# Softmax attention behind the last row maxima in cycles of two steps, with the output projections in parts between the cycles

## The chip, the cores and the metric

The kernel runs on one core of a Trainium2 chip. The metric is the device time of one execution in microseconds (us). A core has engines that run side by side and meet at semaphores: PE (matrix multiply, with weight loads shown apart as PEld), DVE (VectorE), ACT (ScalarE), POOL (GpSimd) and SP, which here issues the DMAs in one list. PE writes to PSUM, eight banks of 128 partitions by 512 float32; operands lie in SBUF.

## The reference

Two attention branches over one input of 2048 tokens and 448 channels, 16 heads of 28 channels, mixed by a gate for each token. All is float32.

```python
x = A_x
g = _sigmoid((x * gate_w).sum(-1, keepdims=True))
a = _A_ref(x, A_wqkv, A_w_phi, A_wo)     # linear attention with a softmax feature map
b = _B_ref(x, B_wqkv, B_wo)              # softmax attention
return g * a + (1 - g) * b

def _B_ref(x, wqkv, wo):
    ...
    scores = jnp.einsum("bhqd,bhkd->bhqk", q, k) * scale
    p = _softmax(scores, axis=-1)
    o = jnp.einsum("bhqk,bhkd->bhqd", p, v)
    return (lambda x, *d: x.transpose(*d))(o, 0, 2, 1, 3).reshape(B, S, D) @ wo
```

The change touches branch B alone, in its last part.

## The kernel before

The first half of the program makes branch A, the queries, keys and values of B, and the first part of the row maxima that the softmax subtracts. The second half is a loop over steps `s` from 0 to 255. The 16 heads go in four groups of four (`g`), the queries in four blocks of 512 (`qb`), the keys in 16 tiles of 128 (`kt`). One step is one `(g, qb, kt)`, with `gq = 4 g + qb` counting groups of 16 steps.

In a step, `scores` makes four score tiles of 128 keys by 512 queries, one for each head, each in a PSUM bank of its own (`st`); ACT takes the exponential of each into a tile `p` in SBUF. `values` of the step before multiplies the four `p` by the values and adds into one bank `pv`: four matmuls of 32 columns each, at four column positions of the array, each stands in the profile as two instructions. While maxima are still to be found, `mx_visit` does a piece of that work in each step: four matmuls `pm`, one ACT and some DVE instructions. It has work in steps 1 to 212. From then on the banks that it held join the rotation, and one, `spare`, is kept for projections, so that six banks remain for scores.

After the last step of a group `finish` normalises in parts that are put into later steps: `f1` copies `pv` (DVE) and gathers the denominators by DMA; `f2`, three steps on, takes the reciprocal and sends it through DRAM to all partitions (`rdb`, `rsb`); `f3`, eight steps on, multiplies (POOL); `f4` splits the result into a high and a low part (POOL, tile `oTb`). For the first three head groups the result goes to DRAM (`od`).

For the last head group, `g = 3`, steps 192 to 255, the output can be made: `project(qb, oT, tl)` makes 128 tokens of the output by 11 matmuls into the spare bank (`pob`): eight read `oL`, the results of the first three groups loaded back from DRAM by `load_out` (the first six read blocks 0 and 1, the next two block 2), and three read `oTb`. DVE adds that to branch A's part in `acc`, and a DMA writes it out. A query block has four projections, in the steps `s + 10` to `s + 13` behind its `finish` (dictionary `mids`). The loads of `oL` are put in steps 200, 222, 242 and 206 (`OUTS`, by query block). `oL` is one buffer for the first three query blocks; the fourth has its own. `acc` has two buffers. Query block 3 is projected at the end, behind the loop's last values, by code that the change leaves alone.

The order on PE, DVE, ACT and POOL is the order in which the program is written; the order of SP's DMAs is made by a planner. SP issues in order: a DMA that waits holds those behind it.

Of the kernel before, what the change touches and what calls it, by code (L numbers as in the profile page):

```python
# [8 lines left out]
F32 = mybir.dt.float32  # L9
# [8 lines left out]
P = 128  # L18
S = 2048
D = 448  # L20
# [3 lines left out]
NG = 4  # L24
NT = S // P
NQ = S // 512
# [2 lines left out]
NU = NG * NQ * 16  # L29
NF = 44  # L30
LOWEST = -3.0e38
OUTS = (200, 222, 242, 206)


def f32(ap):
    return ap.bitcast(F32)
# [3 lines left out]
def gated_mix_kernel(ctx, tc, xT, wqkB, wvB, wvA, wkAT, wqAT, phi, woA, woB,  # L40
# [7 lines left out]
    nc = tc.nc  # L48
# [18 lines left out]
    def ps_mx(nm, d):  # L67
        return ps.tile([P, 2, 512], F32, tag="md" if d and psn[1] == 3 else "mx", name=nm,
                       bufs=1 if d and psn[1] == 3 else 2)
# [18 lines left out]
    gate1 = const.tile([P, NT], F32, name="gate1")  # L88
# [17 lines left out]
    def run(dst, todo):  # L106
        for i, (l, r) in enumerate(todo):
            nc.tensor.matmul(dst, l, r, start=i == 0, stop=i == len(todo) - 1)  # L108
# [48 lines left out]
    acts = []  # L157
# [6 lines left out]
    def take_acts():  # L164
        while acts:
            acts.pop(0)()
# [11 lines left out]
    def mx_tile(tag, nm, bufs):  # L178
        return mxp.tile([P, 512], F32R, tag=tag, name=nm, bufs=bufs)
# [49 lines left out]
    def mx_fin():  # L229
        while mxs["fin"]:  # L230
            mxs["fin"].pop(0)()
# [162 lines left out]
    def normalize1(pool, pn, nm, n):  # L394

        oU = pool.tile([P, n, 512], F32, tag="oU", name=f"oU{nm}", bufs=1 + n)
        for i in range(n):
            (nc.scalar.copy if n == 2 else nc.vector.tensor_copy)(oU[:, i, :], pn[i])  # L398
        den = pool.tile([P, n, 16], F32, tag="den", name=f"den{nm}", bufs=2)
        for i in range(n):  # L400
            nc.sync.dma_start(den[:, i, :], oU[DH:P:32, i, :])
        return oU, den

    def normalize2(pool, oU, den, nm, n, eps):

        if eps:
            nc.vector.tensor_scalar_add(den, den, EPS)
        nc.vector.reciprocal(den, den)
        rd = dr.tile([4, n * 512], F32, tag=f"rd{n}", name=f"rd{nm}", bufs=2)
        rs = pool.tile([P, n, 512], F32, tag="rs", name=f"rs{nm}", bufs=2)  # L410
        for k in range(n):
            nc.sync.dma_start(rd[:, k * 512:(k + 1) * 512], den[:, k, :])
        nc.sync.dma_start(rs.rearrange("p n q -> p (n q)"),
                          rd.unsqueeze(1).to_broadcast([4, 32, n * 512]))
        return oU, rs

    def normalize3(oU, rs, n):

        (nc.gpsimd if n == 1 else nc.vector).tensor_mul(oU, oU, rs)  # L419
        return oU  # L420

    def normalize4(pool, oU, nm, n):

        oTn = []
        for k in range(n):
            oT = pool.tile([P, 2, 512], F32R, tag="oT", name=f"oT{nm}_{k}", bufs=2 * n)
            (nc.scalar.copy if n == 2 else nc.gpsimd.tensor_copy)(oT[:, 0, :], oU[:, k, :])
            nc.gpsimd.tensor_sub(oT[:, 1, :], oU[:, k, :], f32(oT[:, 0, :]))
            oTn.append(oT)
        return oTn  # L430

    def out_passes(oT, c, w, g):
        tt = slice(c, c + P)
        return [(oT[:, 0, tt], w[:, 0, g, :]), (oT[:, 0, tt], w[:, 1, g, :]),
                (oT[:, 1, tt], w[:, 0, g, :])]
# [270 lines left out]
    for i in range(2 * NT + 11):  # L706
        t, q = i, i - NT
# [131 lines left out]
        kst_of[(g, kb)] = load_stack(kst[(4 * g + kb) % 5], k_d[g], kb * 512, (0, 1, 0, 1))  # L839

    NS = NG * NQ * NT
    pv_of, pts, late, mids = {}, {}, {}, {}

    def scores(s, i):

        gq, kt = divmod(s, NT)
        g, qb = divmod(gq, NQ)

        def score(j, st):
            nc.tensor.matmul(st, kst_of[(g, kt // 4)][:, j, (kt % 4) * P:(kt % 4 + 1) * P],  # L850
                             qst_of[gq][:, j, :], start=True, stop=True)

        if s == 0:
            p = at.tile([P, 2, 512], F32, name=f"p{s}_{i}")
            st = ps_mx(f"st{s}_{i}", i)
            for jl in range(2):
                score(2 * i + jl, st[:, jl, :])
            nc.scalar.activation(p, st, AF.Exp, scale=SCALE)
            pts.setdefault(s, []).extend([p[:, 0, :], p[:, 1, :]])
            return  # L860
        sts = []
        for j in (2 * i, 2 * i + 1):
            used.append(free.pop(0))
            sts.append(bank(used[-1], f"st{s}_{j}"))
            score(j, sts[-1])
        for st in sts:
            p = late_p.tile([P, 512], F32, tag="p", name=f"p{s}_{len(pts.get(s, []))}", bufs=8)
            nc.scalar.activation(p, st, AF.Exp, scale=SCALE)  # L868
            pts.setdefault(s, []).append(p)
        if i == 1:  # L870
            a, m = used[:], held[:]
            free.extend([a[0], m[0], a[1], m[1], a[2], a[3], m[2]] if m else a)
            used.clear()
            held.clear()
# [34 lines left out]
    spare = []  # L909

    def bank(i, nm):
        return ps2.tile([P, 512], F32, tag=f"g{i}", name=nm, bufs=1)
# [13 lines left out]
    late_p = ctx.enter_context(tc.tile_pool(name="late", bufs=1, reuse_waits="tile"))  # L926
    woB_s = late_p.tile([P, 2, 4, D], F32R, name="woB_s")
# [51 lines left out]
                             start=kt == 0, stop=kt == NT - 1, tile_position=(0, 32 * j),  # L979
                             skip_group_check=True)  # L980

    def project(qb, oT, tl):

        t = qb * 4 + tl
        acc = acc_of[qb][:, tl, :]
        po = bank(spare[0], f"pob{t}")
        run(po[:, :D], first_passes(qb, tl) + out_passes(oT, tl * P, woB_s, NG - 1))
        nc.vector.scalar_tensor_tensor(acc, po[:, :D], gate1[:, t:t + 1], acc,  # L988
                                       op0=ALU.mult, op1=ALU.add)
        nc.sync.dma_start(out[0, t * P:(t + 1) * P, :], acc)  # L990

    def first_passes(qb, tl):
        o, tt = oL_of[qb], slice(tl * P, (tl + 1) * P)
        return [x for b in range(2) for x in out_passes(o[b], tl * P, woB_s, b)] + [
            (o[2][:, i, tt], woB_s[:, i, 2, :]) for i in range(2)]
# [18 lines left out]
    def finish(gq, s):  # L1014

        st = {}
        g, qb = divmod(gq, NQ)
        last = gq == NG * NQ - 1

        def f1():  # L1020
            st["n"] = normalize1(late_p, [pv_of[gq]], f"b{gq}", 1)

        def f2():
            st["n"] = normalize2(late_p, *st["n"], f"b{gq}", 1, False)

        def f3():
            st["n"] = normalize3(*st["n"], 1)

        def f4():
            st["o"], = normalize4(late_p, st["n"], f"b{gq}", 1)  # L1030
            if g < NG - 1:
                for j in range(4):
                    r = (4 * g + j) * DH
                    nc.sync.dma_start(o_d[r:r + DH, :, qb * 512:(qb + 1) * 512],
                                      f32(st["o"][32 * j:32 * j + DH]))

        if last:
            finish_last(gq)
            return
        f1()  # L1040
        late.setdefault(s + 3, []).append(f2)
        late.setdefault(s + 8, []).append(f3)
        late.setdefault(s + 9, []).append(lambda: acts.append(f4))
        if g == NG - 1:
            for tl in range(4):
                mids[s + 10 + tl] = lambda tl=tl: project(qb, st["o"], tl)

    def finish_last(gq):

# [44 lines left out]
    for s in range(NS + 16):  # L1094
        take_acts()
        if s < NS:
            gq, kt = divmod(s, NT)
            g, qb = divmod(gq, NQ)
            if s in (0, 3):
                load_k(0, 2 + s // 3)  # L1100
            if g + 1 < NG and qb == NQ - 1 and kt % 4 == 2:
                load_k(g + 1, kt // 4)
            if kt == 12 and gq + 1 < NG * NQ:
                load_q(gq + 1)
            if kt == (12 if gq + 1 < 14 else 14) and gq + 1 < NG * NQ - 1:
                load_nm(gq + 1)
            if s in OUTS:
                load_out(OUTS.index(s))
            if g == NG - 1 and kt == 8:
                load_acc(qb)  # L1110
            if s:
                scores(s, 0)
                scores(s, 1)
        if s == NS:
            tail_open()
            tail_fill(3)
        if 0 < s <= NS:
            values(s - 1)
            if s % NT == 0:
                finish(s // NT - 1, s)  # L1120
        if s:
            mx_visit()
        if mxs["f"] == len(flats):
            mx_fin()
        if s in mids:
            mids.pop(s)()
        if mxs["f"] == len(flats) and not spare:
            spare_open()
        if NG * NQ - 1 in nm_of and NG * NQ - 1 in qst_of:
            load_nm(NG * NQ - 1)  # L1130
        for fn in late.pop(s, []):
            fn()
# [68 lines left out]
```

## Time and profile before

| | |
|---|---|
| timed runs, us | 1028.92, 1027.72, 1028.66 (median 1028.66) |
| profiled execution, span, us | 1027.1 |
| median less that span, us | 1.56 |
| PE busy, us | 1018.7 |
| ACT busy, us | 819.4 |
| DVE busy, us | 672.8 |
| POOL busy, us | 245.1 |
| mean granted TensorE clock | 0.998 |

The page has the time of the profiled execution as its span, from the first to the last instruction; the timed runs hold some time around it. A line of the timeline has the start and the length in us, the engine, the line of the kernel, the operation, the tiles as out<-in, the shapes, and the number of instructions merged into it; behind it in brackets is the idle time of that engine before it and what ended that. A line of a table of windows has, for each engine, the busy us and the number of instructions, then the clock, the DMA share and GB/s. Matmuls overlap, so their starts tell more than their lengths.

### The profile page before, as it was taken

The page shows a single profiled execution, that of the slowest core. Times are in us where ns is not written, and L with a number is a line of the kernel's source. Part 1 is how long each engine was busy: PE and PEld are TensorE (multiplying, and loading weights), DVE is VectorE, ACT ScalarE, POOL GpSimd, SP SyncE. Part 2 cuts the span into 40 slices and gives each one's busy share as a digit, 9 for nine tenths or more (in the row PEclk, how much of TensorE's full clock was granted, in tenths as well). Part 3 has the DMA queues.
Part 4 walks back from the last instruction along what each step waited for, and adds up shares of the span by engine and source line. Part 5 has one row for each costly group of instructions (what it writes and reads, how often), then busy time and mean ns, then how long its engine had stood idle before and what let it go on. Part 6 is the DMA issues. An engine that isn't in the chain of part 4 may idle for free.

```text
span 1027.1 us, 17751 instructions
## 1 busy us (share of the span) xinstructions
PE 1018.7 (99%) x6344; PEld 561.2 (55%) x6344; DVE 672.8 (65%) x1335; ACT 819.4 (80%) x1534; POOL 245.1 (24%) x213
## 2 busy tenths in 40 slices
PE   8999999999999999999999999999999999999998
PEld 7878888878779433333333333333333333354545
DVE  5466566997750578888878788787878887710102
ACT  5354445687753899999999999999999999969672
POOL 1226456688436302111011110101201101011010
PEclk9999999999999999999999999999999999999999
DMA  8873110132245703233633123522313355414311
GB/s 294 292 243 116 42 34 19 43 90 79 91 129 122 158 19 83 65 71 68 127 70 77 46 66 81 129 57 50 87 46 74 87 131 138 124 56 127 122 42 54
DMA packets 64025, 98.88 MB, mean 96 GB/s; under 512 B 17952, under 2 KB 24720, under 8 KB 63936
## 3 DMA queue, kind: packets, MB, share of 16 engines
q1 hardware_dynamic: 63936, 97.74, 35.4%
q8 instruction: 50, 0.82, 0.4%
q14 instruction: 39, 0.32, 0.1%
HBM read 69.54 MB, written 27.78 MB: 95 GB/s over the span
## 4 chain that ended last, share of the span: by engine, by line
PE 95%; DVE 2%; DMA 1%; ACT 1%; issue 0%; SPq 0%; DVEq 0%; ACTq 0%
PE st L850 29%; PE pv L977 25%; PE pm L321 9%; PE pqk L108 5%; PE poa L108 4%; PE pk L126 4%; PE pva L126 4%; PE pob L108 3%; PE pq L108 3%; PE pvb L108 2%; PE pmb L284 2%; PE pvb L126 2%; PE pn L532 1%; PE pft L520 1%; PE pkv L475 1%; PE poL L1011 1%
## 5 line engine op out<-in xcount | busy, mean ns | idle before, releaser
L868 ACT ACTIVATE p<-st 128x512 f32<-128x512 f32 x1020 | 525.9, 609 | 29.5 <-PE st L850 27.8
L332 DVE TENSOR_REDUCE part<-pm 128x1 f32<-128x512 f32 x477 | 304.6, 685 | 131.5 <-PE pm L321 124.9
L850 PE MATMUL st<-qst,kst 128*128 128x512 f32 x1024 | 315.6, 430 | 0.5 <-ACT vb L694 0.5
L977 PE MATMUL pv<-p,vb 128*32 128x512 f32 x2048 | 272.8, 605 | 0.2 <-DVE oUb L398 0.2
L850 PEld LDWEIGHTS st<-qst,kst 128*128 128x128 f32 x1024 | 173.1, 187 | 137.4 <-issue 75.8
L321 PEld LDWEIGHTS pm<-kc,qc 28*128 28x128 f32 x848 | 40.5, 181 | 177.8 <-ACT p L868 169.4
L325 ACT ACTIVATE rl<-pm 128x512 f32<-128x512 f32 x212 | 126.9, 599 | 11.1 <-PE pm L321 0.3
L419 POOL TENSOR_TENSOR oUb<-oUb,rsb 128x512 f32<-128x512 f32 x15 | 19.4, 1291 | 469.2 <-DMA rsb<-rdb 375.1
L329 DVE CUSTOM_DVE_ANT_0 rl<-pm,rl 128x512 f32<-128x512 f32 x159 | 108.2, 680 | 0.0
L321 PE MATMUL pm<-kc,qc 28*128 28x512 f32 x848 | 107.1, 495 | 0.0
L289 DVE CUSTOM_DVE_ANT_0 rl<-pmb,rl 128x512 f32<-128x512 f32 x88 | 57.1, 686 | 32.4 <-ACT rl L287 32.4
L977 PEld LDWEIGHTS pv<-p,vb 128*32 128x32 f32 x2048 | 40.3, 108 | 67.6 <-issue 63.4
L988 DVE SCALAR_TENSOR_TENSOR acc<-pob,gate,acc 128x448 f32<-128x448 f32 x12 | 8.2, 683 | 86.2 <-PE pob L108 86.2
L108 PE MATMUL pqk<-XH,wB 128*128 128x512 f32 x192 | 60.8, 404 | 2.3 <-DVE ev L572 2.3
L287 ACT ACTIVATE rl<-pmd 128x1024 f32<-128x1024 f32 x44 | 45.3, 1029 | 8.0 <-ACT z_s L485 2.4
L571 ACT CAST ev<-pqk 128x512 fp32r<-128x512 f32 x28 | 16.0, 589 | 40.2 <-PE pqk L108 35.7
L108 PE MATMUL poa<-woA_s,oTa 128*128 128x448 f32 x192 | 43.2, 374 | 0.0
L108 PEld LDWEIGHTS pqk<-XH,wB 128*128 128x128 f32 x192 | 36.0, 192 | 11.4 <-DVE ev L572 2.7
L572 DVE TENSOR_TENSOR ev<-pqk,ev 128x512 fp32r<-128x512 f32 x28 | 19.0, 690 | 31.6 <-ACT ev L571 31.5
L108 PEld LDWEIGHTS poa<-woA_s,oTa 128*128 128x128 f32 x192 | 35.0, 188 | 5.8 <-issue 2.8
L195 POOL TENSOR_TENSOR kc<-kc,kd 28x512 fp32r<-28x512 f32 x12 | 15.4, 1282 | 95.7 <-DMA kc<-qkd 59.4
L126 PE MATMUL pk<-wkA_s,XH 128*128 128x448 f32 x128 | 37.9, 377 | 0.0
(155 smaller groups left out, 1186.6 us busy)
## 6 DMA issues: line engine op xcount, KB each, us to landing
qkd<-ev SPq DMA_DIRECT2D x28, 512.0 KB
qst<-qkd SPq DMA_DIRECT2D x64, 224.0 KB
kst<-qkd SPq DMA_DIRECT2D x64, 224.0 KB
od<-oTb SPq DMA_DIRECT2D x48, 112.0 KB
rsa<-rda SPq DMA_DIRECT2D x8, 512.0 KB
rsb<-rdb SPq DMA_DIRECT2D x15, 256.0 KB
kc<-qkd SPq DMA_DIRECT2D x64, 56.0 KB
gad<-ga SPq DMA_DIRECT2D x16, 224.0 KB
```

What stands on the lines that cost most here:

```text
L108: nc.tensor.matmul(dst, l, r, start=i == 0, stop=i == len(todo) - 1)
L126: nc.tensor.matmul(dst[:, :n], l, r, start=i == 0, stop=i == len(todo) - 1, skip_group_check=True)
L284: nc.tensor.matmul((pb if j < 2 else pd)[:, j % 2, :], qc[js, qt * P:(qt + 1) * P], kc[js, :], start=True, stop=True, tile_position=(32 * ...
L287: nc.scalar.activation(rl, pd, AF.Relu)
L289: nc.vector.tensor_tensor_reduce(rl[:, i, :], pb[:, i, :], rl[:, i, :], 1.0, LOWEST, ALU.add, ALU.max, part[:, col + i:col + i + 1])
L321: nc.tensor.matmul(pm[j], mxs[("qc", gq)][js, qt * P:(qt + 1) * P], mxs[("kc", g, kb)][js, :], start=True, stop=True, tile_position=(32 * ...
L325: nc.scalar.activation(rl, pm[kb], AF.Relu if kb < 3 else AF.Copy)
L329: nc.vector.tensor_tensor_reduce(r, pm[j], r, 1.0, LOWEST, ALU.add, ALU.max, part[:, col + j:col + j + 1])
L332: nc.vector.tensor_reduce(part[:, col + j:col + j + 1], pm[j], AX.X, ALU.max)
L850: nc.tensor.matmul(st, kst_of[(g, kt // 4)][:, j, (kt % 4) * P:(kt % 4 + 1) * P], qst_of[gq][:, j, :], start=True, stop=True)
L868: nc.scalar.activation(p, st, AF.Exp, scale=SCALE)
L977: nc.tensor.matmul(pv[32 * j:32 * j + 32, :], vb[kt // 8][:, kt % 8, 4 * g + j, :], pt[j], start=kt == 0, stop=kt == NT - 1, tile_position ...
```

## The change

From step `TWO` = 213 on, which is the first without work on maxima, steps go in pairs. In an odd step the scores of that step and of the next are made, eight in a row; then come the values of the step before it, and then, in the even step, the values of the odd one. The exponentials of even steps go to tiles that held queries and keys for the maxima (`qc`, `kc`), so that there are 16 tiles `p`.

A projection is cut into two halves, of six and of five matmuls into the same bank. They stand in a list, `halves`, with the earliest step for each, and are taken in even steps behind the values: one in a step up to 232, two in a step from 234 on. The earliest step is that behind `f4`, or three behind the load of `oL`. Those loads move from steps 222 and 242 to 233 and 243. For groups that end behind step 213, `f2`, `f3` and `f4` come 2, 5 and 6 steps behind the group's end instead of 3, 8 and 9.

```diff
-OUTS = (200, 222, 242, 206)
+OUTS = (200, 233, 243, 206)
...
+    TWO = NG * NQ * 16 - NF + 1
...
-        for st in sts:
-            p = late_p.tile([P, 512], F32, tag="p", name=f"p{s}_{len(pts.get(s, []))}", bufs=8)
+        for j, st in enumerate(sts, 2 * i):
+            if s < TWO or s % 2:
+                p = late_p.tile([P, 512], F32, tag="p", name=f"p{s}_{j}", bufs=8)
+            else:
+                tag = "qc" if s % 4 and j < 3 else "kc"
+                p = f32(mx_tile(tag, f"p{s}_{j}", 3 if tag == "qc" else 5))
...
-    def project(qb, oT, tl):
+    halves, po_b = [], {}
+
+    def project(qb, st, tl, half):
...
-        po = bank(spare[0], f"pob{t}")
-        run(po[:, :D], first_passes(qb, tl) + out_passes(oT, tl * P, woB_s, NG - 1))
-        nc.vector.scalar_tensor_tensor(acc, po[:, :D], gate1[:, t:t + 1], acc,
+        if half == 0:
+            po_b[t] = bank(spare[0], f"pob{t}")
+        todo = first_passes(qb, tl) + out_passes(st["o"], tl * P, woB_s, NG - 1)
+        for i, (l, r) in enumerate(todo):
+            if i // 6 == half:
+                nc.tensor.matmul(po_b[t][:, :D], l, r, start=i == 0, stop=i == 10,
+                                 skip_group_check=True)
+        if half == 0:
+            return
+        nc.vector.scalar_tensor_tensor(acc, po_b.pop(t)[:, :D], gate1[:, t:t + 1], acc,
                                        op0=ALU.mult, op1=ALU.add)
...
-        late.setdefault(s + 3, []).append(f2)
-        late.setdefault(s + 8, []).append(f3)
-        late.setdefault(s + 9, []).append(lambda: acts.append(f4))
+        d2, d3, d4 = (3, 8, 9) if s < TWO else (2, 5, 6)
+        late.setdefault(s + d2, []).append(f2)
+        late.setdefault(s + d3, []).append(f3)
+        late.setdefault(s + d4, []).append(lambda: acts.append(f4))
         if g == NG - 1:
-            for tl in range(4):
-                mids[s + 10 + tl] = lambda tl=tl: project(qb, st["o"], tl)
+            halves.extend((max(s + d4 + 1, OUTS[qb] + 3), lambda tl=tl, half=half: project(qb, st, tl, half))
+                          for tl in range(4) for half in range(2))
...
-            if s:
-                scores(s, 0)
-                scores(s, 1)
+            for z in ([s] if s < TWO else [s, s + 1][:NS - s] if s % 2 else []):
+                if z:
+                    scores(z, 0)
+                    scores(z, 1)
...
-        if s in mids:
-            mids.pop(s)()
+        for _ in range(0 if s % 2 else 1 if s < 234 else 2):
+            if halves and halves[0][0] <= s:
+                halves.pop(0)[1]()
```

More of the change, by code (lines that the diff above doesn't have):

```diff
@@ L841, in gated_mix_kernel @@
     NS = NG * NQ * NT
-    pv_of, pts, late, mids = {}, {}, {}, {}
+    TWO = NG * NQ * 16 - NF + 1
+    pv_of, pts, late = {}, {}, {}
     def scores(s, i):
```

## The prediction

> **What bounds the kernel now.** I read the page's first and fourth parts, then the chain of waits cut to the end of the run, where every edit lies, then the timeline there.
>
> ```profile
> PE 1018.7 (99%) x6344; PEld 561.2 (55%) x6344; DVE 672.8 (65%) x1335; ACT 819.4 (80%) x1534; POOL 245.1 (24%) x213
> PE 95%; DVE 2%; DMA 1%; ACT 1%; issue 0%; SPq 0%; DVEq 0%; ACTq 0%
> by line: PE st L850 34.9%; PE pv L977 33.2%; PE pob L108 19.9%; PE poL L1011 4.8%; PE poL L1080 1.7%; PE pm L321 1.5%; PE pr L1065 0.7%; PE pd L1055 0.7%; DVE oUb L398 0.5%; DVE acc L1081 0.5%; issue 0.1%
> ```
>
> The third line is the chain from 880 us on: scores (`st`), values (`pv`) and projections (`pob`), all on PE. A busy PE need not be full, so next the timeline of plain steps, with scores and ACT's exponentials also cut out singly:
>
> ```profile
> 898.08 1.06 PE L977 MATMUL pv<-p,vb 128*32 128x512 f32 x8
> 898.53 0.61 PE L977 MATMUL pv<-p,vb 128*32 128x512 f32 x4
> 899.08 0.76 PEld L850 LDWEIGHTS st<-qst,kst 128*128 128x128 f32 x4 [0.84 <-issue]
> 899.08 1.19 PE L850 MATMUL st<-qst,kst 128*128 128x512 f32 x4
> 899.41 0.39 PE L850 MATMUL st<-qst,kst 128*128 128x512 f32 x1
> 899.64 0.40 PE L850 MATMUL st<-qst,kst 128*128 128x512 f32 x1
> 899.88 0.40 PE L850 MATMUL st<-qst,kst 128*128 128x512 f32 x1
> 900.20 1.06 PE L977 MATMUL pv<-p,vb 128*32 128x512 f32 x8
> 899.67 0.60 ACT L868 ACTIVATE p<-st 128x512 f32<-128x512 f32 x1
> ```
>
> A step is 2.12 us (898.08 to 900.20): values 1.00 (to 899.08), scores 1.12. The scores' starts show where time is lost: 0.33 from the first to the second, 0.23 to each further one, and 0.32 from the fourth to the first value. In a run of scores each costs 0.23; so going from values (column tiles of 32) to scores costs 0.10 and back 0.09. The values are two lots of four that run side by side, 0.45 apart (898.08, 898.53), and the second needs 0.55 (to 899.08), though a lot of such width needs less inside a run. The nearest run of column tiles is `pn`, half as wide:
>
> ```profile
> 198.16 0.59 PE L532 MATMUL pn<-fT,KV 112*64 112x256 f32 x3
> 198.58 0.39 PE L532 MATMUL pn<-fT,KV 112*64 112x256 f32 x2
> ```
>
> These are its second and fourth lot: 0.42 for two lots of 256, so 0.43 (they stand at 0.215 each) for one of 512. Leaving the values thus costs 0.55 - 0.43 = 0.12. Does ACT bound instead? The steps with a projection:
>
> ```profile
> 905.44 1.89 PE L108 MATMUL pob<-woB_s,oL 128*128 128x448 f32 x8
> 907.78 1.08 PE L850 MATMUL st<-qst,kst 128*128 128x512 f32 x4
> 908.27 2.07 ACT L868 ACTIVATE p<-st 128x512 f32<-128x512 f32 x4 [2.29 <-PE st L850]
> 908.79 1.06 PE L977 MATMUL pv<-p,vb 128*32 128x512 f32 x8
> 909.79 1.90 PE L108 MATMUL pob<-woB_s,oL 128*128 128x448 f32 x8
> ```
>
> Four exponentials take 2.07, the last 0.60 alone, so they follow each other at 0.49; four are 1.96 of a 2.12 step. PE bounds, with ACT 8% behind it. A projection step is 4.35 (905.44 to 909.79): projection 2.34, scores 1.01 (no switch of tiles before them), values 1.00; ACT idles 2.29. So the stretch from step 213 on is 42 steps of 2.12 plus 12 projections of 2.23, all PE.
>
> **The change part by part.**
>
> *Eight scores, then two steps' values.* This removes one pair of switches per two steps. There are 21 cycles (213/214 to 253/254; 255 stays alone). Without waits a cycle's scores take 0.33 + 6 x 0.23 + 0.32 = 2.03 to 2.05, its values 0.45 + 2 x 0.43 + 0.55 = 1.86: 3.91 instead of 4.24.
>
> But the change adds a wait: `spare` leaves six banks in rotation, so the seventh and eighth score reuse the banks of the first and second and wait for their exponentials. The nearest row is a score that waits for ACT today:
>
> ```profile
> 892.75 0.60 ACT L325 ACTIVATE rl<-pm 128x512 f32<-128x512 f32 x1
> 893.40 0.19 PEld L850 LDWEIGHTS st<-qst,kst 128*128 128x128 f32 x1 [0.21 <-ACT rl L325]
> 893.82 0.16 PEld L977 LDWEIGHTS pv<-p,vb 128*32 128x32 f32 x8 [0.24 <-issue]
> ```
>
> ACT ends at 893.35, the weight load starts 0.05 later, the values 0.42 after that. In a cycle the first exponential starts 0.59 after the first score (899.08 to 899.67), the second ends at 0.59 + 0.49 + 0.60 = 1.68, the eighth's load starts at 1.73, the values at 2.15. Behind the waiting score stand only the values of the step before, ready long since. The seventh is released at 0.59 + 0.60 + 0.05 = 1.24, about when its load is due: no cost. So a cycle is 2.15 + 1.86 = 4.01, a gain of 0.23. After a projection all starts come 0.10 earlier: 2.05 + 1.86 + 2.34 = 6.25 against 2.12 + 4.35 = 6.47, gain 0.22. Bounds: 0.33 with no wait; 0.10 if lots stay 0.45 apart and the wait costs 0.08 more. The second half of the values needs the fourth exponential, at 0.59 + 3 x 0.49 + 0.60 + 0.05 = 2.71; it is due at 2.15 + 0.88 = 3.03. ACT's eight take 3.92 of 4.01. I take 0.225 x 21 = 4.7.
>
> *Values of a new group* stand behind eight scores instead of four. At step 240 they waited:
>
> ```profile
> 970.00 1.19 PE L850 MATMUL st<-qst,kst 128*128 128x512 f32 x4
> 970.61 0.69 DVE L398 COPY oUb<-pv 128x512 f32<-128x512 f32 x1 [5.99 <-PE st L850]
> 971.35 0.16 PEld L977 LDWEIGHTS pv<-p,vb 128*32 128x32 f32 x8 [0.60 <-DVE oUb L398]
> ```
>
> 1.35 from the scores instead of 1.12: 0.2 that goes. Next late behind it are the eight scores, 2.15.
>
> *Projections in two parts.* A part of six or five matmuls stands between values and scores: it pays the 0.10 of leaving the values, which the scores after it then save. Net 0, and the eight projections from step 236 on run both parts together, 2.34 as now. *More p tiles* (16 for 8): ACT's idle time in the rows is put down to `st`, not to a missing tile: 0.
>
> *The loads of `oL`.* Projections now run later and in longer rows, and `oL` is one buffer: the second query block's is loaded when the first's eighth half (step 232) has read it, and used at step 236. Before, 13 steps lay between; now two cycles. The same point before (920.86 is the first score behind the fourth projection, T in what follows):
>
> ```profile
> 920.44 0.60 SPq L942 DMA_DIRECT2D oL<-od  x1
> 920.86 1.09 PE L850 MATMUL st<-qst,kst 128*128 128x512 f32 x4
> 921.77 0.33 SPq L990 DMA_DIRECT2D out_dram<-acc  x1
> 922.15 0.58 SPq L942 DMA_DIRECT2D oL<-od  x1
> 922.78 1.20 SPq L945 DMA_DIRECT2D oL<-od  x2
> 924.96 0.42 SPq L948 DMA_DIRECT2D oL<-od  x1
> 928.75 0.47 SPq L968 DMA_DIRECT2D acc<-gad  x1
> 930.38 0.34 SPq L412 DMA_DIRECT2D rdb<-denb  x1
> 934.11 0.58 SPq L413 DMA_DIRECT2D rsb<-rdb  x1
> ```
>
> The built order of the changed program puts SP's issues here as: `oL` block 0, `out`, block 1, first part of block 2, `acc` (896 KB, for the third query block), then the other four parts of block 2 (346 KB). That `acc` takes the buffer of the first query block, so it waits until the `out` before it has landed, and the four parts stand behind it on SP. `out` is issued at T + 0.9 behind 512 KB:
>
> ```profile
> 924.00:925.00 1.00, 1.00 (x10) 0.16 (x9) 0.00 (x0) 1.00 (x4) 0.00 (x0) 1.00 1.07 364
> 928.00:929.00 1.00, 1.00 (x10) 0.16 (x8) 0.07 (x1) 1.00 (x3) 0.00 (x0) 1.00 0.33 102
> ```
>
> (the last number is GB/s in that us). At 364 the 736 KB take 2.1 us, so `out` has not landed before 923, about T + 2; the whole set of 1.7 MB ends about 929, T + 8. I take the middle for `out`, T + 5. Then `acc` issues (0.5), and the four parts at 0.47 each. How long a small load behind `acc` takes, the rows show: `acc` at 928.75, `rdb` behind it has landed when `rsb` issues, 934.11: 5.4 after `acc`. The parts thus land from T + 10.4 on; with 346 KB at the 364 GB/s above, to T + 11.4. They are due at T + 3.91 + 4.01 (two cycles, the first behind a projection) + 0.3 + 5 x 0.2 (six matmuls ahead of them) = T + 9.2. I take 10.9: a stall of 1.7 us, bounds 0 and 2.9. Behind it on PE stands everything.
>
> *The normalisation of group 14* is due at step 248 rather than 250, and its reciprocal stands behind the eighth projection's sum on DVE (step 242). With T now behind that projection, `rdb` issues about T + 1.3, behind 736 KB, and lands about 5.4 after that first load as above: T + 5.0. From `rsb` to the end of POOL's work:
>
> ```profile
> 942.02 1.29 POOL L419 TENSOR_TENSOR oUb<-oUb,rsb 128x512 f32<-128x512 f32 x1 [39.16 <-DMA qst<-nm]
> 944.06 1.29 POOL L428 TENSOR_TENSOR oTb<-oUb,oTb 128x512 fp32r<-128x512 f32 x1
> 893.69 0.60 SPq L413 DMA_DIRECT2D rsb<-rdb  x1
> 899.52 1.30 POOL L419 TENSOR_TENSOR oUb<-oUb,rsb 128x512 f32<-128x512 f32 x1 [38.20 <-DMA rsb<-rdb]
> ```
>
> 7.9 (from 934.11, among big loads) or 5.8 (893.69 to 899.52, nearly alone), and 3.3 of POOL: T + 14.1 to 16.2. Due at T + 3.91 + 2 x 4.01 + 0.3 + 9 x 0.2 = T + 14.0. So 0.1 to 2.2; most of the neighbours are ahead of it here, so I stay near the lower: 0.2.
>
> **Sum.** -4.7 - 0.2 + 1.7 + 0.2 = -3.0 on the profiled span of 1027.1: 1024.1. The median of the timed runs, 1028.66, lies 1.56 above that span; added again: 1025.7.
>
> **The rivals.**
>
> *The loads come in time.* If `out` lands by T + 3.7 and the parts pass among `acc`'s pieces, they are issued by T + 3.7 + 0.5 + 4 x 0.47 = T + 6.1 and have until 9.2. Gain 4.9 alone: 1023.8. Against it: `rdb` behind `acc` didn't pass. [...] No row here shows a landing of `out`. Chance 0.23.
>
> *The scores wait more than they save.* With six banks the cycle is tied to ACT, which has 0.09 to spare. If loads, releases and lots cost at the bad bound, the gain is 0.10 x 21 = 2.1; with 0.2 and the stalls of 1.9 the time is 1028.3, no change. For it: a load released late costs 0.42 to the values, where an unhindered one costs 0.55 in the open; against: every link has a row. Chance 0.18.
>
> *Slower: SP stands behind `acc`.* One wait in SP's list holds four loads that PE needs. It decides where the parts land later than T + 9.2 + 4.9 = T + 14.1. If `acc` and the parts move at the 102 GB/s of the last us above, 1.24 MB take 12 us from about T + 6: T + 18, a stall of 8.8 and a time of 1028.66 - 4.9 + 8.8 = 1032.6. For it: small parts did move at that rate; against: `acc` itself is landed within 5.4. Chance 0.10.
>
> *Nothing changes because ACT bounds* after all would need 0.53 for an exponential; the four in 2.07 rule it out but for 0.02.
>
> **How the numbers follow.** The forecast, gain 4.9 and stalls of 0.7 to 2.9, has 0.47, with 1024.4 to 1026.7. About 0.2% (2.1 us) is what a measurement can tell from no change: faster is below 1026.6. From the forecast 0.44, from the first rival 0.22: 0.66 faster. Same: 0.03 from the forecast, 0.01 of the first rival, 0.16 of the second, 0.02 of ACT, 0.01 of the third's milder end: 0.23. Slower: 0.02 of the second, 0.09 of the third: 0.11. The range leaves out the third rival and the best end of the first: 1022.9 to 1028.4.
>
> **What would show it.** In the profile after: cycles of about 4.01 (eight scores 2.15 with the eighth's load released by ACT, values 1.86); a projection's first part of six near 1.3; ACT idle about 1.3 in cycles with a part; at step 236 a wait of PE for `oL` of 1 to 3 us, and SP's `acc` issued about T + 5; near none at step 248. Wrong would be: cycles near 4.2, a lot pitch of 0.45 or more, a wait at each seventh score, or a stall at step 236 of over 5.

## The result: a little slower, with cycles as predicted and two stalls that take more than they gave

| | before | after |
|---|---|---|
| median of 13 runs, us | 1028.53 (1027.20 to 1029.09) | 1029.65 (1028.43 to 1036.45) |
| ratio, 95% interval | | 1.0021 [1.0012, 1.0029] |
| profiled execution: span, us | 1027.1 | 1026.8 (its time 1028.63) |
| from the first score of step 213 to that of step 255, us (profile) | 116.22 (892.65 to 1008.87) | 117.03 (891.61 to 1008.64) |

The forecast was 1025.7, in a range of 1022.9 to 1028.4: the sign is wrong. The kernel also spreads more than before. The last row of the table is the stretch in which every edit lies; what comes ahead of it moves by 1 to 3 us from execution to execution in all kernels here, so profiles are compared by the stretch.

First the timeline of PE after the change, at the first cycles:

```profile
895.84 2.24 PE L851 MATMUL st<-qst,kst 128*128 128x512 f32 x8
898.00 1.92 PE L982 MATMUL pv<-p,vb 128*32 128x512 f32 x16
899.86 2.24 PE L851 MATMUL st<-qst,kst 128*128 128x512 f32 x8
...
903.88 1.50 PE L998 MATMUL pob<-woB_s,oL 128*128 128x448 f32 x6
905.22 2.13 PE L851 MATMUL st<-qst,kst 128*128 128x512 f32 x8
```

By the starts, eight scores take 2.16, sixteen value instructions 1.86, a cycle 4.02, a projection's first part 1.34, the scores behind it 2.05. The waits of weight loads from 890 us on name what the eighth score waits for:

```profile
PEld st L851 <- ACT p L873: 5.7, 20, 0.3
```

Twenty times, once a cycle, an exponential releases it. So the cycle is the predicted one (4.01, 2.15, 1.86). Now step 236, PE and then SP in the timeline, and the granted clock in windows of 1 us (the number after the engines; then the DMA share and GB/s):

```profile
949.25 1.49 PE L998 MATMUL pob<-woB_s,oL 128*128 128x448 f32 x6
952.68 1.18 PE L998 MATMUL pob<-woB_s,oL 128*128 128x448 f32 x2 [1.95 <-DMA oL<-od]
...
954.78 2.58 PE L851 MATMUL st<-qst,kst 128*128 128x512 f32 x8
957.29 1.92 PE L982 MATMUL pv<-p,vb 128*32 128x512 f32 x16
```

```profile
943.25 0.63 SPq L950 DMA_DIRECT2D oL<-od  x1
946.05 0.34 SPq L973 DMA_DIRECT2D acc<-gad  x1
...
948.03 0.42 SPq L953 DMA_DIRECT2D oL<-od  x1
```

```profile
952.00:953.00 1.00, 0.32 (x1) 0.29 (x1) 0.00 (x0) 0.00 (x0) 0.00 (x0) 0.80 0.03 10
953.00:954.00 1.00, 1.00 (x3) 0.83 (x3) 0.00 (x0) 0.00 (x0) 0.00 (x0) 0.50 0.00 0
...
956.00:957.00 1.00, 1.00 (x6) 0.75 (x4) 0.00 (x0) 1.00 (x4) 0.00 (x0) 1.00 0.41 152
```

SP waits 2.2 us at `acc`, with four loads of `oL` behind it. The seventh matmul was due 1.30 behind the first, at 950.55, and starts at 952.68: 2.13 of waiting. Then the clock is 0.5 from 952.6 to 956.0. The projection takes 5.53 (949.25 to 954.78) where an unhindered one takes 2.34, and the next scores 2.51 where they take 2.05: 3.65 in all, so the low clock adds 1.52 to the wait. Last, step 248, PE and POOL:

```profile
985.95 2.04 PE L998 MATMUL pob<-woB_s,oL 128*128 128x448 f32 x8
988.20 0.68 PE L998 MATMUL pob<-woB_s,oTb 128*128 128x448 f32 x2 [0.22 <-POOL oTb L427]
989.56 0.48 PE L998 MATMUL pob<-woB_s,oTb 128*128 128x448 f32 x1 [0.68 <-POOL oTb L428]
989.87 1.31 PE L851 MATMUL st<-qst,kst 128*128 128x512 f32 x5
...
986.18 1.29 POOL L419 TENSOR_TENSOR oUb<-oUb,rsb 128x512 f32<-128x512 f32 x1 [51.45 <-DMA rsb<-rdb]
```

3.92 instead of 2.34: 1.58 lost to the normalisation of group 14. Both stalls cost 5.23, and the stretch is 0.81 longer than before; without them it would be 4.42 shorter.

### The profile page after: what moved, and what is told of

It reads as the page before. It is cut to its first block, busy times and chain, and to the rows that moved or that the text cites. A ratio compares the mean times of both kernels' runs of the same rounds, so it can differ in the third digit from the quotient of the medians.

```text
span 1026.8 us, 17727 instructions
## 1 busy us (share of the span) xinstructions
PE 1016.3 (99%) x6344; PEld 566.2 (55%) x6344; DVE 672.8 (66%) x1335; ACT 816.9 (80%) x1534; POOL 244.5 (24%) x213
## 4 chain that ended last, share of the span: by engine, by line
PE 94%; DMA 2%; DVE 2%; ACT 0%; issue 0%; POOL 0%; POOLq 0%; SPq 0%; DVEq 0%; ACTq 0%
PE st L851 28%; PE pv L982 24%; PE pm L321 9%; PE pqk L108 5%; PE poa L108 4%; PE pk L126 4%; PE pva L126 4%; PE pob L998 3%; PE pq L108 3%; PE pvb L108 2%; PE pmb L284 2%; PE pvb L126 2%; PE pn L532 1%; PE pft L520 1%; PE pqk L634 1%; PE pkv L475 1%
## 5 line engine op out<-in xcount | busy, mean ns | idle before, releaser
L982 PE MATMUL pv<-p,vb 128*32 128x512 f32 x2048 | 268.4, 604 | 0.0
L851 PEld LDWEIGHTS st<-qst,kst 128*128 128x128 f32 x1024 | 175.5, 188 | 124.1 <-issue 55.5
L982 PEld LDWEIGHTS pv<-p,vb 128*32 128x32 f32 x2048 | 43.8, 108 | 68.9 <-issue 65.6
```

Of the source, the lines that this page charges most:

```text
L982: nc.tensor.matmul(pv[32 * j:32 * j + 32, :], vb[kt // 8][:, kt % 8, 4 * g + j, :], pt[j], start=kt == 0, stop=kt == NT - 1, tile_position ...
```

## The experiments

Three sets of runs; within a set, all share the runs of the kernel before. Its medians were 1028.97 (first four), 1029.13 (next four) and 1028.41 (last two). e5 and e6 have five timed runs each, the others 9 to 12. The theory: the cycles give what was predicted; SP's order and short distances between a transfer and its use take it back, and the clock behind an idle PE adds to that. Rivals: the cycles give less than their profile says; loads come too late whatever stands in SP's list; long rows of projections in the late steps are what costs.

| run | median, us | ratio to before, 95% interval | stretch, us |
|---|---|---|---|
| e1_acc_later | 1026.81 | 0.9980 [0.9970, 0.9989] | 114.67 |
| e2_recip_first | 1028.97 | 1.0003 [0.9995, 1.0012] | 116.57 |
| e3_both | 1026.45 | 0.9980 [0.9972, 0.9988] | 113.88 |
| e4_whole_early | 1029.26 | 0.9998 [0.9989, 1.0007] | 116.70 |
| e5_slack | 1025.48 | 0.9965 [0.9952, 0.9977] | 111.79 |
| e6_seven_banks | 1022.52 | 0.9931 [0.9918, 0.9945] | 109.43 |
| e7_eight_p_tiles | 1029.73 | 1.0007 [0.9999, 1.0016] | 117.41 |
| e9_single_steps | 1028.85 | 0.9996 [0.9987, 1.0005] | 116.10 |
| e8_fill | 1030.75 | 1.0016 [1.0002, 1.0029] | 116.31 |
| e10_changed_again | 1030.38 | 1.0012 [1.0001, 1.0022] | 118.43 |

**One stall at a time.** First the large `acc` load of query block 2 six steps later, so that it no longer stands in front of the `oL` loads.

```diff
-            if g == NG - 1 and kt == 8:
+            if g == NG - 1 and kt == (14 if qb == 2 else 8):
```

> The changed kernel with the load of acc for the third query block written six steps later (step 238 instead of 232), so that it stands behind all parts of oL on SP. Theory A (the parts of block 2 of oL are late because they stand behind acc, which waits for out to land; the idle PE then runs at half clock for 3.4 us): the wait at step 236, 2.1 us, goes, and the half clock with it, together 3.7; the wait at step 248 (1.6) stays. About 1026, with a smaller spread between runs. Rival B (two cycles are too short for 1.7 MB in any order): a wait of over 1 us stays at step 236, the half clock with it, and the time is above 1028.

Measured 2.2 below before. The PE timeline at step 236:

```profile
950.02 0.88 PE L998 MATMUL pob<-woB_s,oL 128*128 128x448 f32 x3
951.07 0.88 PE L998 MATMUL pob<-woB_s,oL 128*128 128x448 f32 x3 [0.17 <-DMA oL<-od]
952.67 0.78 PE L998 MATMUL pob<-woB_s,oL 128*128 128x448 f32 x2 [0.72 <-DMA oL<-od]
953.29 0.77 PE L998 MATMUL pob<-woB_s,oTb 128*128 128x448 f32 x3
```

The projection takes 3.87 (to the scores at 953.89), 1.53 too long instead of 3.19, and the clock stays at 1.00. With the low clock the stall was 3.65, so more than half of it goes with the order on SP, but not all of it, as theory A had expected. Then the reciprocal of group 14 one step earlier, alone and with the former:

```diff
         d2, d3, d4 = (3, 8, 9) if s < TWO else (2, 5, 6)
+        if gq == 14:
+            d2 = 1
```

> The changed kernel with the reciprocal of group 14 one step earlier (241), ahead of the eighth projection's sum on DVE, so that the normalisation's DMAs go ahead of the loads of oL on SP. Theory A: the wait at step 248 (1.6 us) goes, that at step 236 stays with its half clock: about 1028. Rival B (POOL is late because its own transfer takes that long): the wait at step 248 stays over 1 us, 1029.6.

> Both of the edits before. Theory A: no wait of PE on a load or on POOL from step 213 on, the gain of the cycles alone, 4.9 less than before: 1023.6 to 1024.5, and runs as close together as those of before. Rival B: waits of 2 to 4 us stay, 1026 or more. Rival C (the cycles gain less than their starts show, the rest is lost elsewhere): no waits and still above 1026.

With the reciprocal alone the waits at step 248 are gone, but in this profile the wait for `oL` at step 236 is 3.0, with the clock at 0.5 behind it, and the time is that of before:

```profile
954.84 1.07 PE L998 MATMUL pob<-woB_s,oL 128*128 128x448 f32 x2 [2.97 <-DMA oL<-od]
```

With both edits the expected 1023.6 to 1024.5 were missed (1026.45). Waits for `oL` are left, all at step 236:

```profile
953.50 0.88 PE L998 MATMUL pob<-woB_s,oL 128*128 128x448 f32 x3 [0.54 <-DMA oL<-od]
955.29 0.77 PE L998 MATMUL pob<-woB_s,oL 128*128 128x448 f32 x2 [0.91 <-DMA oL<-od]
```

Nothing stands in front of these loads on SP now, and they still come late: two cycles are too short for `oL`, at least with `acc` right behind it (SP issues `acc` at 948.79, behind the last part at 948.20, and packets of its size move between 951.3 and 957.0, beside the last of `oL`). So the order on SP is part of the cause. How much of the rest is the distance and how much `acc` beside the loads, these runs don't separate; e5 changes both.

**Whole projections, earlier.** Both parts in each even step, so that the first query block is done at step 224 and the second projected from 232 on.

```diff
-OUTS = (200, 233, 243, 206)
+OUTS = (200, 225, 239, 206)
...
-        for _ in range(0 if s % 2 else 1 if s < 234 else 2):
+        for _ in range(0 if s % 2 else 2):
```

> The changed kernel with both halves of a projection in each even step from the start (four steps 218 to 224, 232 to 238, 248 to 254) and the loads of oL at steps 225 and 239, so that at least three cycles lie between the last use of oL and the next first. Theory A: no waits, 1023.6 to 1024.5, the same as with both edits; spreading the halves gains nothing on PE. Rival C: cutting the projections is what gains, and cycles with a whole projection lose 0.5 each: 1026 or more.

A miss: the stall only moved. Group 13 ends at step 224, and its normalisation was not ready at 232; PE, then SP:

```profile
942.24 1.90 PE L998 MATMUL pob<-woB_s,oL 128*128 128x448 f32 x8
946.42 0.67 PE L998 MATMUL pob<-woB_s,oTb 128*128 128x448 f32 x2 [2.28 <-POOL oTb L427]
947.77 0.74 PE L998 MATMUL pob<-woB_s,oTb 128*128 128x448 f32 x1 [0.68 <-POOL oTb L428]
948.31 3.25 PE L851 MATMUL st<-qst,kst 128*128 128x512 f32 x8
...
931.24 0.37 SPq L412 DMA_DIRECT2D rdb<-denb  x1
932.10 0.34 SPq L973 DMA_DIRECT2D acc<-gad  x1
937.56 0.59 SPq L413 DMA_DIRECT2D rsb<-rdb  x1
```

`rdb` is issued behind the seven loads of `oL`, and takes until 937.5 with `acc` beside it. The clock is 0.5 here too, from 947.6 to 951.0, and the eight scores' row is 3.25 instead of 2.13. The cycles with whole projections take 6.25 as elsewhere: cutting projections in parts neither gains nor costs.

**Room for every transfer.** From e4, the second query block moves to steps 234 to 240, its `oL` is loaded behind `rdb`, the reciprocals of groups 13 and 14 come a step earlier, and both late `acc` loads later.

```diff
-OUTS = (200, 225, 239, 206)
+OUTS = (200, 227, 243, 206)
...
+        if gq > 12:
+            d2, d3, d4 = (1, 5, 6)
...
-            halves.extend((max(s + d4 + 1, OUTS[qb] + 3),
+            halves.extend((max(s + d4 + 1 + 2 * (qb == 1), OUTS[qb] + 3),
...
-            if g == NG - 1 and kt == 8:
+            if g == NG - 1 and kt == (14 if qb == 2 else 11 if qb == 3 else 8):
```

> Both parts of a projection run in each even step, the second query block's start at step 234, its oL is loaded from step 227, the large accumulator loads come later, and the reciprocals of groups 13 and 14 one step earlier: each project has four cycles or more between its inputs' start and its use. Theory (the cycles gain the predicted 4.9, the changed kernel lost it in the two stalls and the half clock behind them): no wait of the tensor engine over 0.3 us after step 213, no half clock there, stretch from step 213 to 255 at 116.2 - 4.8 = 111.4 us, time 4.9 below before: ratio 0.9952, about 1024.1. Rival 1 (in most executions the cycles gain only about 2, as the first two repairs' median of 1026.5 would say if nothing was left over): ratio 0.998, stretch near 114. Rival 2 (a stall moves once more, to group 13's or 14's normalisation): a wait of 1 to 3 us at step 234 or 248, ratio 0.998 to 1.000.

No wait of PE shows in the stretch, and its clock is 1.00 over all of it (busy time of the windows view: PE, PEld, DVE, ACT, POOL):

```profile
892.23:1004.03 111.80, 111.80 (x641) 64.78 (x638) 12.19 (x22) 85.03 (x170) 9.57 (x9) 1.00 0.31 88
```

4.43 below before's stretch; in the median 3.65, with an interval of 2.4 to 4.9. The expected 111.4 was missed by 0.4, most of it one cycle of 4.30 (from step 227) whose first exponential starts late. The changed kernel has the same at this place (5.30 where its like takes 5.03); the cause was not followed further.

**What the pairing is worth, and what it needs.** From e5, three single edits: steps of one; one bank more in the rotation; eight tiles `p` instead of sixteen.

```diff
 e9: -            for z in ([s] if s < TWO else [s, s + 1][:NS - s] if s % 2 else []):
     +            for z in [s]:
 e6: -        spare.append(free.pop())
     +        spare.append(True)
     ...
     -            po_b[t] = bank(spare[0], f"pob{t}")
     +            free.append(free.pop(0))
     +            po_b[t] = bank(free[-1], f"pob{t}")
 e7: -            if s < TWO or s % 2:
     ...
     +            p = late_p.tile([P, 512], F32, tag="p", name=f"p{s}_{j}", bufs=8)
```

> As e5_slack, but with steps of four scores and four values as before the change; the new times of loads, reciprocals and projections stay. Theory (all of the gain is the pairing: one set of switches less per two steps, 0.23 for each of 21 cycles): the stretch is 116.0 to 116.5 us as in the kernel before, time 4.9 above e5_slack, about 1029, ratio 0.9995 to 1.0005. Rival (the new times of loads and projections bring part of it): 1026 to 1027.5.

> As e5_slack, with the seventh bank in the rotation of scores and projections instead of kept for projections alone, so that the eighth score reuses the bank of the first. Theory (the eighth score's wait for the second exponential costs 0.10 a cycle): its load is released by the first exponential, 0.59 + 0.60 + 0.05 = 1.24 us after the first score, before it is due; scores take 2.03 to 2.05 instead of 2.15, a plain cycle 3.91 to 3.95 instead of 4.01; 21 cycles give 1.3 to 2.1 us: about 1022.4, ratio 0.9935 to 0.994. Rival (the eight exponentials, 3.92 at 0.49 each, already set the cycle): cycle stays at 4.0, the wait moves to the seventh or first score or to the values, time within 0.5 of e5_slack.

> As e5_slack, with eight p tiles instead of sixteen behind step 213 (undoes 'more p tiles'). Theory: the fifth exponential of a cycle needs the tile that the first values of that cycle read; these start 2.15 and have read it by about 3.05, instead of 2.55 when the exponential is due, so ACT loses about 0.45 and the plain cycle goes to 4.4 to 4.5 us; the twelve cycles with a projection have the time to spare. Nine plain cycles: +4.0 us against e5_slack (0.8 if a tile is free after half of the values). Rival (tiles do not matter, the cycle is the tensor engine's): as e5_slack within 0.3.

Without the pairs the stretch is 116.10, that of the kernel before (116.22): all of the gain is the pairs, 4.31 in the profile and 3.4 in the median. With the seventh bank, PE and ACT in the timeline:

```profile
898.16 2.11 PE L851 MATMUL st<-qst,kst 128*128 128x512 f32 x8
900.20 1.93 PE L982 MATMUL pv<-p,vb 128*32 128x512 f32 x16
902.05 2.14 PE L851 MATMUL st<-qst,kst 128*128 128x512 f32 x8
...
898.76 7.45 ACT L873 ACTIVATE p<-st 128x512 f32<-128x512 f32 x15 [0.58 <-PE st L851]
```

Scores take 2.04, the plain cycle 3.89, and the line of the eighth score's wait is gone from the waits. The fifteen exponentials follow each other at 0.49 ((7.45 - 0.60) / 14) without a break: eight are 3.92, so in plain cycles ACT is now as full as PE. The stretch falls by another 2.36 (1.3 to 2.1 were expected; 0.38 of it is the cycle from step 227, now 3.92), the median to 1022.52, below both kernels. With eight tiles, again PE and ACT:

```profile
898.56 2.89 PE L851 MATMUL st<-qst,kst 128*128 128x512 f32 x8
...
903.23 2.89 PE L851 MATMUL st<-qst,kst 128*128 128x512 f32 x8
...
902.52 4.03 ACT L869 ACTIVATE p<-st 128x512 f32<-128x512 f32 x8 [0.65 <-PE pv L978]
```

ACT now waits 0.65 for the values that read the tiles, and the plain cycle is 4.67 (expected 4.4 to 4.5). The whole gain is lost. The tiles cost nothing, but without them pairs are no better than single steps.

**The clock, and the spread.** The changed kernel with ten unused matmuls in the gap at step 236, and the changed kernel again beside it:

```diff
+            if t == 4 and i == 6 and half:
+                for f in range(FILL):
+                    nc.tensor.matmul(po_f[:, :D], *todo[0], start=True, stop=True,
+                                     skip_group_check=True)
```

> The changed kernel, with ten matmuls of 448 columns that nobody reads (about 0.21 us each, into a bank of scores that is free) put between the sixth and the seventh matmul of the projection at step 236, so that the tensor engine works while it would wait for oL. The loads stay late. Theory (the half clock behind that stall is set off by the tensor engine's idle time, and costs about 1.7 us on top of the wait): granted clock 1.00 from 950 to 960 us, the cycle from step 235 takes 8.2 to 8.7 us instead of 9.55 and the next 6.25 instead of 6.71, time 1.3 to 1.7 below the changed kernel. Rival (the low clock has another cause, or falls at that time anyway): the half clock stays, the cycles stay at 9.5 to 10 and 6.7.

> The changed kernel as it is, beside e8_fill on the same chip: 1029.0 to 1030.3 by its first runs.

Step 236 with the fill, in the timeline and in a window of 1 us (lines of that kernel are some numbers on):

```profile
949.52 1.50 PE L1004 MATMUL pob<-woB_s,oL 128*128 128x448 f32 x6
950.85 2.20 PE L1001 MATMUL pof<-woB_s,oL 128*128 128x448 f32 x10
953.65 0.75 PE L1004 MATMUL pob<-woB_s,oL 128*128 128x448 f32 x2 [0.60 <-DMA oL<-od]
...
954.85 2.12 PE L852 MATMUL st<-qst,kst 128*128 128x512 f32 x8
956.90 1.92 PE L983 MATMUL pv<-p,vb 128*32 128x512 f32 x16
```

```profile
954.00:955.00 1.00, 1.00 (x6) 0.94 (x6) 0.00 (x0) 0.00 (x0) 0.00 (x0) 1.00 0.00 0
```

The load came later here (the seventh matmul is 2.83 behind its due time, not 2.13), so the cycle is 9.34 and not the expected 8.2 to 8.7; but the clock stays at 1.00, the next scores take 2.05 and the next cycle 6.24: the low clock is gone with the idle time. In the median nothing was gained (the expected 1.3 to 1.7 were missed), and the runs spread from 1027.6 to 1033.2; the profile is of one of the shorter (1028.17). A likely reason is in the second profile of the changed kernel, PE and windows:

```profile
949.54 1.49 PE L998 MATMUL pob<-woB_s,oL 128*128 128x448 f32 x6
955.37 1.08 PE L998 MATMUL pob<-woB_s,oL 128*128 128x448 f32 x2 [4.33 <-DMA oL<-od]
...
957.37 2.56 PE L851 MATMUL st<-qst,kst 128*128 128x512 f32 x8
```

```profile
954.00:955.00 1.00, 0.00 (x0) 0.00 (x0) 0.00 (x0) 0.00 (x0) 0.00 (x0) 1.00 0.06 23
...
956.00:957.00 1.00, 1.00 (x5) 0.87 (x3) 0.00 (x0) 0.00 (x0) 0.00 (x0) 0.50 0.00 0
```

SP issued as before (the last part at 948.48), but the wait is 4.53 (955.37 against a due 950.84). In the last us of the wait the DMA share is 0.06, one engine of sixteen, at 23 GB/s. The trace's single packets do not name their engine, but the last ones follow each other without overlap, as on one engine: four of 7,168 bytes from 952.6 to 954.1, a size that here only `acc` has, and then eleven of 2,048 bytes, those of `oL`, to 955.03. By that order a part of `oL` waited here not for `acc`'s issue alone but for `acc`'s bytes ahead of it on one engine. With 1.40 of low clock the stall costs 5.93 in this execution, against 3.65 in the first. How late that engine is differs between the two profiles. That the time of the other runs varies with it, and that the fill was too short in the long ones, would fit; no long run of the fill has a profile that shows it.

## Why the prediction was wrong

The sum had four terms and one omission.

- *The cycles, -4.7:* the mechanism was right, and nearly the size. The links came out as worked out (2.16, 1.86, 4.02; 6.25 with a projection; the release by the second exponential), and e5 against e9 gives -4.3 for the pairs. Two cycles gain less than the others: the first, which takes 4.24 against 4.31 before, and the one from step 227, 4.30.
- *Values of a new group, -0.2:* right; the steps with that wait took 4.47 before (970.00 to 974.47) against 4.24 for two plain ones, and the cycle that now holds these values, with a projection, takes 6.27 (967.73 to 974.00), as others do.
- *The parts of projections and the p tiles, 0:* right. A projection in parts adds 1.02 and 1.22 to its two cycles, 2.24 together. The tiles were costed at nothing without saying what they prevent, which e7 puts at 0.66 for each plain cycle.
- *The loads of `oL`, +1.7, bounds 0 to 2.9:* the mechanism was right step by step, with `acc` issued at T + 4.7 (forecast 5), the last packets at T + 11.1 (10.9) and the due time T + 9.2. This term was mis-sized: the stall is 3.65 in the first profile and 5.93 in the second, against 1.7. The wait itself was 2.13, inside the bounds, and 4.53, outside them (last packets at T + 13.4); the landing, taken from one row, is not a fixed number. (By the page's sizes the four parts hold 352 KB, not 346; that changes nothing.)
- *The normalisation of group 14, +0.2, bounds 0.1 to 2.2:* 1.58 and 0.75 in the two profiles. `rdb` (T + 1.3) and `rsb` (T + 4.8) came as forecast; the time from `rsb` to POOL was 7.4 (978.77 to 986.18), near the row among big loads (7.9) and not the row taken (5.8). SP's list still had four loads of `oL` to issue behind `rsb`, so the first was the nearer row, though there POOL's wait is put down to another load (`qst`). With nothing behind `rsb` on SP for 16 us the link took 4.9 in the kernel before (977.87 to 982.79). That the loads behind it make the difference was not tried by itself.
- *The omission:* behind the wait at step 236 PE came back at half clock (0.5 for 3.4 us in both profiles), which cost another 1.52 and 1.40. The prediction priced a wait at its length.

With the measured terms the stretch closes: -4.43 (e5) + 3.65 + 1.58 = +0.80 against a measured +0.81, and for the second execution -4.43 + 5.93 + 0.75 = +2.25 against +2.21. Against the forecast of -3.0 the first profile is 3.8 off: 0.5 from the cycles and the new group (4.43 for 4.9), 0.4 from the wait for `oL`, 1.5 from the clock and 1.4 from the normalisation. So the clock, which the sum left out, and the normalisation failed most there; in the second profile it was the landing of `oL` (2.8 too small).

Of the rivals, that the loads come in time is what e5 made true by other distances; it counted on `out` by T + 3.7, and `acc`, which waits for `out`, was issued at T + 4.7. That the scores wait more than they save was wrong; their wait is 0.1 a cycle, as e6 shows. The slower one had the right place and the right mechanism, SP and the loads behind `acc`. Its price of 8.8 was not reached in either profile; the run of 1036.45 has none, and by e5's gain it lost, as an estimate, 12.4 in places that are not known (1036.45 - 1028.53 + 4.43). Its point was put too late: landing at T + 14.1 was to decide, and a wait of 2.13, with 1.52 of low clock and 1.58 at step 248, already took the gain. Its chance of 0.10 was low, though a median 1.1 above before is less than the 2.1 us that the prediction counts as a change. Of its signs of being wrong, a stall of over 5 at step 236 came in the second profile (5.93), and the forecast of nearly none at step 248 failed in both (1.58 and 0.75, inside the term's bounds).

## What to carry to other kernels

Before a consumer is moved closer to a transfer, list what the issuing queue and the DMA engines hold ahead of it: a large load of no urgency in front of a small urgent one cost its issue here (0.34 us for `acc`), its wait (2.2) and, by the order of the packets in e10, its bytes ahead of the last of `oL`. Price a wait of PE at its length plus what the clock did behind such a wait (1.52 and 1.40 here), and take the landing from rows with the same company, at their worse end. A gain of a few tenths a cycle over 21 cycles is real (4.43 in e5), but one late load eats it (5.93 in e10); give each transfer a cycle or two to spare first, then look at the wait that is left in the cycle itself, as the seventh bank did.

## What the runs showed of the hardware that was not expected

- From the end of some waits of PE on, the granted clock was 0.5 for 3.4 us: with idle times of 1.95 in the changed kernel (952.6 to 956.0), 2.97 in e2 (955.0 to 958.4), 2.28 and 0.68 close together in e4 (947.6 to 951.0) and 4.33 in e10 (955.1 to 958.5). It stayed at 1.00 behind 0.54 and 0.91 in e3, and behind 0.60 in e8. The length of a wait did not decide alone: near the start of the program the clock stayed at 1.00 behind one of 2.43 in e9, and was 0.50 behind one of 1.87 in e5. What else decides was not shown. The wait and the clock a little later (the number after the engines), first e9, then e5:

```profile
22.46 0.73 PE L108 MATMUL pqk<-XH,wB 128*128 128x512 f32 x2 [2.43 <-DVE ev L572]
24.00:25.00 1.00, 1.00 (x6) 0.84 (x5) 0.00 (x0) 0.00 (x0) 0.00 (x0) 1.00 1.02 371
...
22.68 0.73 PE L108 MATMUL pqk<-XH,wB 128*128 128x512 f32 x2 [1.87 <-DVE ev L572]
24.00:25.00 1.00, 1.00 (x4) 0.81 (x3) 0.00 (x0) 0.00 (x0) 0.00 (x0) 0.50 0.98 371
```

- Nearly the same issue times did not give the same landing. The last part of `oL`, issued at T + 6.7 in the first profile of the changed kernel (948.03) and at T + 6.9 in the second (948.48), came at 952.4 and at 955.0. By the order of the packets in e10, which follow each other as on one engine, four of `acc` went ahead of the last eleven of `oL` (952.6 to 955.03).
